# One query matmul per tile, one bank for the first half of K, three halvings of the second half, result matmuls at the head of the next value loop

## Chip, cores, metric

One core of one Trainium2 chip. The metric is the device time of one execution in microseconds (us), the median of several runs on the same chip.

## The reference

```python
B, H, Sq, Skv, Dh = 8, 32, 1, 4096, 128          # q, k, v in bf16
scale = q.shape[-1] ** -0.5
scores = jnp.einsum('bhqd,bhkd->bhqk', q, k) * scale
attn = softmax(scores, axis=-1)
return jnp.einsum('bhqk,bhkd->bhqd', attn, v)
```

Attention of a single query row for 256 heads: each head reads its own K and V (1 MB each) once and does little with them.

## The kernel before

32 tiles of 8 heads. In a tile a partition holds 256 of a head's rows (16 partitions per head), so K and V of a tile are 128 x 32768 bf16, 8.39 MB each. Three buffers of that size hold K and V in turn. VectorE multiplies K by the query in place and halves the rows by adding; TensorE sums what is left with an identity matrix into a PSUM bank of 512 columns, VectorE reduces the bank to scores. ScalarE makes the weights, and TensorE multiplies them with V in a loop that runs one tile later. The parts that the change touches:

```python
    def q_prep(t):
        x, p0 = divmod(t * G, P)                          # q_all: 128 partitions
        qh = ps_q.tile([G, D], F32, name="qh", tag="qp")
        nc.tensor.matmul(qh[:], lhsT=ident[:, p0 : p0 + G], rhs=q_all[:, x, :], ...)
        qg = q_pool.tile([G, D], BF16, name="qg", tag="qg")
        nc.scalar.activation(out=qg[:], in_=qh[:], func=ACT.Copy)
        qp = ps_q.tile([P, D], F32, name="qp", tag="qp")
        nc.tensor.matmul(qp[:], lhsT=heads[:]..., rhs=qg[:], start=True, stop=True)
        qb = q_pool.tile([P, 1, D], BF16, name="qb", tag="qb")
        nc.scalar.activation(out=qb[:, 0, :], in_=qp[:], func=ACT.Copy)
    ...
    def width_of(t, u):                                   # u: quarter of K
        return D // 4 if u >= NU // 2 and 0 < t < NT - 3 else D // 2
    def product(t, lo, hi):
        nc.vector.tensor_tensor(out=part, in0=part, in1=qb[:].to_broadcast(...), op=ALU.mult)
        nc.vector.tensor_tensor(... 0 : D // 2 ... + D // 2 : D ...)
        if width_of(t, lo // UC) < D // 2:
            nc.vector.tensor_tensor(... 0 : D // 4 ... + D // 4 : D // 2 ...)
    def sum_over_d(t, u):                                 # one bank per quarter of K
        ps = ps_s.tile([P, UC, DS], F32, name="ps", tag="ps")
        n = width_of(t, u) // DS
        for s in range(n):
            nc.tensor.matmul(ps[:], lhsT=ident[:], rhs=kt[:, u * UC : (u + 1) * UC, s * DS : (s + 1) * DS], ...)
    ...
        for t in range(NT):                               # cut: the steady tiles
            product(t, 0, 2 * Q)
            ...
            result_of(t - 2)
            q_prep(t + 2)
            sum_over_d(t, 0); sum_over_d(t, 1)
            product(t, 2 * Q, 3 * Q); sum_over_d(t, 2)
            scores_of(t, 0); scores_of(t, 1)
            product(t, 3 * Q, C); sum_over_d(t, 3)
            scores_of(t, 2)
            values_loop(t - 1)
            load("k", t + 1); load("v", t)
            scores_of(t, 3); weights_of(t); copy_of(t - 1)
```

## Time and profile before

| | before |
|---|---|
| time, median | 1251.86 us (1251.5 to 1251.9) |
| span of the profiled run | 1250.2 us |
| VectorE, TensorE, ScalarE busy | 82%, 63%, 13% |
| load queue busy | 99.5% of 16 DMA engines |
| one steady tile | 38.7 us |

The prediction shows the lines that carry this. Two more kinds matter for what follows, and the prediction passed over them. The first are small rows of the list of DMA queues (queue and kind: packets, MB, share of 16 engines' time): beside the loads (q1), the programs of the engines are fetched by DMA while they run. Kernel before:

```profile
q8 instruction: 15, 0.25, 0.1%
q14 instruction: 9, 0.07, 0.0%
```

0.1% of the time, 24 packets. The second is the end of the stream in windows of 1 us (columns: window, its length, busy time and instructions of each engine, TensorE clock, DMA share, GB/s). Kernel before:

```profile
1244.00:1245.00 1.00, 0.61 (x8) 0.21 (x8) 0.00 (x0) 0.00 (x0) 0.00 (x0) 1.00 0.50 183
1245.00:1246.00 1.00, 0.40 (x4) 0.10 (x4) 0.00 (x0) 0.12 (x1) 0.00 (x0) 1.00 0.16 56
1246.00:1247.00 1.00, 0.98 (x18) 0.98 (x18) 0.00 (x0) 0.48 (x1) 0.00 (x0) 1.00 0.01 4
```

The DMA share is a mean over 16 engines, so one engine at work is 0.06. The loads do not stop at once: the share falls over 3 us, and the last V rows land only when the last engine is done.

### The profile page before, as it was taken

The page shows a single profiled execution, that of the slowest core. Times are in us where ns is not written, and L with a number is a line of the kernel's source. Part 1 is how long each engine was busy: PE and PEld are TensorE (multiplying, and loading weights), DVE is VectorE, ACT ScalarE, POOL GpSimd, SP SyncE. Part 2 cuts the span into 40 slices and gives each one's busy share as a digit, 9 for nine tenths or more (in the row PEclk, how much of TensorE's full clock was granted, in tenths as well). Part 3 has the DMA queues.
Part 4 walks back from the last instruction along what each step waited for, and adds up shares of the span by engine and source line. Part 5 has one row for each costly group of instructions (what it writes and reads, how often), then busy time and mean ns, then how long its engine had stood idle before and what let it go on. Part 6 is the DMA issues. An engine that isn't in the chain of part 4 may idle for free. (4 is left out here: it accounts for less than half of the span.)

```text
span 1250.2 us, 10842 instructions
## 1 busy us (share of the span) xinstructions
PE 786.8 (63%) x3116; PEld 299.6 (24%) x3116; DVE 1021.9 (82%) x495; ACT 166.1 (13%) x433; POOL 4.5 (0%) x24
## 2 busy tenths in 40 slices
PE   3366567666576655766558665577655776556755
PEld 1122123222232222322223222222222222212222
DVE  7887987878977789777798777987779877798783
ACT  0111011111011110111101111011110111101111
POOL 1000000000000000000000000000000000000000
PEclk9987788777888778877788777887778878779867
DMA  9999999999999999999999999999999999999997
GB/s 405 436 436 435 434 436 432 436 430 428 426 437 436 429 435 434 434 435 436 436 434 432 424 437 437 432 430 428 436 437 434 430 433 434 430 435 421 427 446 329
DMA packets 11432, 537.33 MB, mean 430 GB/s; under 512 B 1808, under 2 KB 2064, under 8 KB 2320
## 3 DMA queue, kind: packets, MB, share of 16 engines
q1 hardware_dynamic: 11072, 536.94, 99.5%
q8 instruction: 15, 0.25, 0.1%
q10 hardware_dynamic: 336, 0.07, 0.0%
q14 instruction: 9, 0.07, 0.0%
HBM read 536.94 MB, written 0.07 MB: 430 GB/s over the span
## 5 line engine op out<-in xcount | busy, mean ns | idle before, releaser
L191 DVE TENSOR_TENSOR kt<-kt,qb 128x8192 bf16<-128x8192 bf16 (+1 forms) x99 | 560.9, 5665 | 146.6 <-DMA kt<-in_k_dram 139.9
L211 PE MATMUL ps<-kt,ident 128*128 128x512 bf16 x800 | 278.4, 511 | 389.9 <-DVE kt L199 299.7
L294 PE MATMUL av<-vt,w 128*32 x1740 | 425.5, 397 | 4.6
L194 DVE TENSOR_TENSOR kt<-kt 128x4096 bf16<-128x4096 bf16 (+1 forms) x99 | 288.8, 2917 | 3.4
L294 PEld LDWEIGHTS av<-vt,w 128*32 x1740 | 173.4, 100 | 262.4 <-issue 119.5
L211 PEld LDWEIGHTS <-ident 128*128 128x128 bf16 x800 | 95.7, 120 | 565.4 <-issue 527.9
L223 DVE TENSOR_REDUCE sc<-ps 128x64 f32<-128x512 f32 x128 | 85.3, 685 | 54.0 <-PE ps L211 54.0
L248 ACT ACTIVATE e<-sc,nmax 128x256 bf16<-128x256 f32 x32 | 16.3, 508 | 706.7 <-DVE nmax L242 706.7
L255 ACT ACTIVATE w<-e,mine 128x256 bf16<-128x256 bf16 x256 | 105.6, 495 | 1.1
L199 DVE TENSOR_TENSOR kt<-kt 128x2048 bf16<-128x2048 bf16 x56 | 68.6, 1225 | 1.9
L351 ACT ACTIVATE comb<-av 32x512 bf16<-32x512 f32 (+1 forms) x32 | 18.8, 586 | 329.0 <-PEq L284 321.4
L280 PE MATMUL av<-vt,w 128*32 128x512 bf16 x116 | 47.2, 499 | 14.6 <-issue 13.1
L371 PE MATMUL op<-comb,pick 32*16 32x128 bf16 (+1 forms) x128 | 12.1, 213 | 20.7 <-ACT comb L351 20.7
L280 PEld LDWEIGHTS av<-vt,w 128*32 128x32 bf16 x116 | 6.9, 100 | 55.2 <-issue 55.2
L177 PE MATMUL qp<-qg,heads 8*128 8x128 bf16 x32 | 7.0, 217 | 16.7 <-ACT qg L175 16.7
L371 PEld LDWEIGHTS <-pick 32*16 32x16 bf16 (+1 forms) x128 | 8.7, 83 | 27.7 <-issue 27.3
L322 PE MATMUL av<-vt,w 128*32 128x512 bf16 x188 | 13.7, 418 | 2.3 <-DMA vt<-in_v_dram 2.3
L235 DVE TENSOR_REDUCE pmax<-sc 128x1 f32<-128x256 f32 x32 | 13.4, 420 | 1.1
L175 ACT ACTIVATE qg<-qh 8x128 bf16<-8x128 f32 x32 | 8.5, 266 | 33.5 <-PE qh L171 33.5
L171 PE MATMUL qh<-q_all,ident 128*8 128x128 bf16 x32 | 7.2, 225 | 8.7 <-DMA q_all<-in_q_dram 8.3
L179 ACT ACTIVATE qb<-qp 128x128 bf16<-128x128 f32 x32 | 8.9, 278 | 9.7 <-PE qp L177 9.7
L237 DVE TENSOR_SCALAR spread<-same,pmax 128x32 f32<-128x32 f32 x32 | 7.7, 242 | 1.1
(31 smaller groups left out, 47.7 us busy)
## 6 DMA issues: line engine op xcount, KB each, us to landing
kt<-in_k_dram SPq DMA_DIRECT2D x4, 4096.0 KB, 24.3
kt<-in_k_dram SPq DMA_DIRECT2D x4, 2048.0 KB, 13.0
vt<-in_v_dram SPq DMA_DIRECT2D x1, 4096.0 KB, 33.9
vt<-in_v_dram SPq DMA_DIRECT2D x1, 2048.0 KB, 38.5
vt<-in_v_dram SPq DMA_DIRECT2D x1, 1024.0 KB, 40.5
vt<-in_v_dram SPq DMA_DIRECT2D x1, 512.0 KB, 41.3
vt<-in_v_dram SPq DMA_DIRECT2D x31, 25.8
kt<-in_k_dram SPq DMA_DIRECT2D x29, 28.3
```

Source lines behind the costliest of these rows:

```text
L191: nc.vector.tensor_tensor(out=part, in0=part, in1=qb[:].to_broadcast([P, hi - lo, D]), op=ALU.mult)
L194: nc.vector.tensor_tensor(out=part[:, :, 0 : D // 2], in0=part[:, :, 0 : D // 2], in1=part[:, :, D // 2 : D], op=ALU.add,)
L199: nc.vector.tensor_tensor(out=part[:, :, 0 : D // 4], in0=part[:, :, 0 : D // 4], in1=part[:, :, D // 4 : D // 2], op=ALU.add,)
L211: nc.tensor.matmul(ps[:], lhsT=ident[:], rhs=kt[:, u * UC : (u + 1) * UC, s * DS : (s + 1) * DS], start=(s == 0), stop=(s == n - 1),)
L223: made = nc.vector.tensor_reduce(out=scs[t][:, u * UC : (u + 1) * UC], in_=sums.pop((t, u))[:], axis=AX.X, op=ALU.add)
L248: nc.scalar.activation(out=e[:], in_=sc[:], func=ACT.Exp, bias=nmax[:, 0:1], scale=scale, accum_out=esums[t // R][:, t % R : t % R + 1],)
L255: nc.scalar.activation(out=w[:, :, g, :], in_=e_g, func=ACT.Copy, scale=mine[:, 0, g : g + 1])
L280: pe.matmul(av, lhsT=wf[:, i * nw : (i + 1) * nw], rhs=vf[:, i * nv : (i + 1) * nv], **how)
L294: pe.matmul(av, lhsT=wf[:, bass.ds(ow + i * nw, nw)], rhs=vf[:, bass.ds(ov + i * nv, nv)], start=False, stop=False,)
L322: nc.tensor.matmul(avs[t][j * AG : (j + 1) * AG, :], lhsT=w[:, i, :, :], rhs=vt[:, c0 : c0 + CB, :], start=(i < TG), stop=(j not in group[ ...
L351: nc.scalar.activation(out=comb[0:n, :, :], in_=av[0:n, :, :], func=ACT.Copy)
L371: nc.tensor.matmul(ops[n][:], lhsT=pick[0:e, m, r, :], rhs=comb[0:e, m, :], start=(r == 0 and m == 0), stop=(r == R - 1 and m == CB - 1 an ...
```

## The change

Its intent: fewer matmuls and copies (one query matmul instead of two, two sums per quarter of the second half of K instead of four, one PSUM bank and one reduction for the whole first half), in exchange for one more add per quarter, and a TensorE that starts the sums of the next tile without the result matmuls ahead of them. The query of a tile is also made one tile ahead instead of two. The diff, cut to its core:

```diff
-    q_n = q.rearrange("b h o d -> (b h o) d").rearrange("(x p) d -> p x d", p=P)
+    q_n = q.rearrange("b h o d -> (b h o) d").rearrange("(x p) d -> p x d", p=QP)      # QP = 32
-    heads = consts.tile([G, G, PH], BF16, name="heads")
+    heads = consts.tile([QP, QP, PH], BF16, name="heads")
     def q_prep(t):
-        ... matmul with ident, copy to qg, matmul with heads, copy to qb
+        x, h0 = divmod(t * G, QP)
+        qp = ps_q.tile([P, D], F32, name="qp", tag="qp")
+        nc.tensor.matmul(qp[:], lhsT=heads[:, h0 : h0 + G, :].rearrange("h g x -> h (g x)"), rhs=q_all[:, x, :], ...)
+        ... copy to qb
-        return D // 4 if u >= NU // 2 and 0 < t < NT - 3 else D // 2
+        return D // 8 if lo >= C // 2 and 0 < t < NT - 3 else D // 2
     def product(t, lo, hi):
+        n = D
+        while n > width_of(t, lo):
+            n //= 2
             nc.vector.tensor_tensor(
+                out=part[:, :, 0:n], in0=part[:, :, 0:n], in1=part[:, :, n : 2 * n], op=ALU.add
-    def sum_over_d(t, u):
+    def sum_over_d(t, lo, hi):
+        ds = BANK // (hi - lo)                             # 512 columns, whatever the rows
+        n = width_of(t, lo) // ds
-        e = o_pool.tile([P, C], BF16, name="e", tag="e")
+        e = o_pool.tile([P, C], BF16, name="e", tag="ec")
-        comb = o_pool.tile([P, CB, D], BF16, name="comb", tag="comb")
+        comb = o_pool.tile([P, CB, D], BF16, name="comb", tag="ec")
         with tc.tile_critical() as loop:
+            if t > 0:
+                result_of(t - 1)
...                                                        # w_last in the scores pool, the loop of tiles
```

More of the change, by code (lines that the diff above doesn't have):

```diff
@@ L43 @@
     scale = float(D) ** -0.5
-    UC = 64
-    DS = 512 // UC
-    NU = C // UC
+    BANK = 512
     CB = 4
@@ L49 @@
     NQ = NT // R
+    QP = 32
     TB = 32
@@ L53 @@
     assert (NV - 2 * EDGE) % LOOP == 0
-    assert LAST % CB == 0 and TG * AG == P and NH % P == 0 and P % G == 0 and TB % PH == 0 and C % CB == 0
-    q_n = q.rearrange("b h o d -> (b h o) d").rearrange("(x p) d -> p x d", p=P)
+    assert LAST % CB == 0 and TG * AG == P and NH % QP == 0 and QP % G == 0 and TB % PH == 0 and C % CB == 0
+    q_n = q.rearrange("b h o d -> (b h o) d").rearrange("(x p) d -> p x d", p=QP)
     o_n = out.rearrange("b h o d -> (b h o) d").rearrange("(n u x) d -> n x u d", u=OB, x=RG)
@@ L62 @@
     consts = ctx.enter_context(tc.tile_pool(name="consts", bufs=1))
-    q_pool = ctx.enter_context(tc.tile_pool(name="q_pool", bufs=3))
+    q_pool = ctx.enter_context(tc.tile_pool(name="q_pool", bufs=2))
     w_pool = ctx.enter_context(tc.tile_pool(name="w_pool", bufs=2))
@@ L72 @@
     ps_z = ctx.enter_context(tc.tile_pool(name="ps_z", bufs=1, space=bass.MemoryType.PSUM))
-    q_all = consts.tile([P, NH // P, D], BF16, name="q_all")
+    q_all = consts.tile([QP, NH // QP, D], BF16, name="q_all")
     ident = consts.tile([P, P], BF16, name="ident")
@@ L81 @@
     )
-    heads = consts.tile([G, G, PH], BF16, name="heads")
+    heads = consts.tile([QP, QP, PH], BF16, name="heads")
     nc.gpsimd.memset(heads[:], 0.0)
     nc.gpsimd.affine_select(
-        out=heads[:], in_=heads[:], pattern=[[-1, G], [0, PH]], compare_op=ALU.not_equal,
+        out=heads[:], in_=heads[:], pattern=[[-1, QP], [0, PH]], compare_op=ALU.not_equal,
         fill=1.0, base=0, channel_multiplier=1,
@@ L128 @@
     )
-    w_last = consts.tile([P, LAST, RG], BF16, name="w_last")
-    nc.gpsimd.memset(w_last[:], 0.0)
     loads = {}
@@ L168, in q_prep @@
     def q_prep(t):
-        x, p0 = divmod(t * G, P)
-        qh = ps_q.tile([G, D], F32, name="qh", tag="qp")
+        x, h0 = divmod(t * G, QP)
+        qp = ps_q.tile([P, D], F32, name="qp", tag="qp")
         nc.tensor.matmul(
-            qh[:], lhsT=ident[:, p0 : p0 + G], rhs=q_all[:, x, :], start=True, stop=True
-        )
-        qg = q_pool.tile([G, D], BF16, name="qg", tag="qg")
-        nc.scalar.activation(out=qg[:], in_=qh[:], func=ACT.Copy)
-        qp = ps_q.tile([P, D], F32, name="qp", tag="qp")
-        nc.tensor.matmul(qp[:], lhsT=heads[:].rearrange("g h x -> g (h x)"), rhs=qg[:], start=True, stop=True)
+            qp[:], lhsT=heads[:, h0 : h0 + G, :].rearrange("h g x -> h (g x)"), rhs=q_all[:, x, :],
+            start=True, stop=True,
+        )
         qb = q_pool.tile([P, 1, D], BF16, name="qb", tag="qb")
@@ L180, in q_prep, with width_of @@
         qbs[t] = qb
-    def width_of(t, u):
-        return D // 4 if u >= NU // 2 and 0 < t < NT - 3 else D // 2
+    def width_of(t, lo):
+        return D // 8 if lo >= C // 2 and 0 < t < NT - 3 else D // 2
     def product(t, lo, hi):
@@ L193, in product, with scores_of @@
         )
-        nc.vector.tensor_tensor(
-            out=part[:, :, 0 : D // 2], in0=part[:, :, 0 : D // 2],
-            in1=part[:, :, D // 2 : D], op=ALU.add,
-        )
-        if width_of(t, lo // UC) < D // 2:
+        n = D
+        while n > width_of(t, lo):
+            n //= 2
             nc.vector.tensor_tensor(
-                out=part[:, :, 0 : D // 4], in0=part[:, :, 0 : D // 4],
-                in1=part[:, :, D // 4 : D // 2], op=ALU.add,
+                out=part[:, :, 0:n], in0=part[:, :, 0:n], in1=part[:, :, n : 2 * n], op=ALU.add
             )
     sums = {}
-    def sum_over_d(t, u):
+    def sum_over_d(t, lo, hi):
         kt = loads["k", t]
-        ps = ps_s.tile([P, UC, DS], F32, name="ps", tag="ps")
-        n = width_of(t, u) // DS
+        ps = ps_s.tile([P, BANK], F32, name="ps", tag="ps")
+        ds = BANK // (hi - lo)
+        n = width_of(t, lo) // ds
         for s in range(n):
             nc.tensor.matmul(
-                ps[:], lhsT=ident[:],
-                rhs=kt[:, u * UC : (u + 1) * UC, s * DS : (s + 1) * DS],
+                ps[:], lhsT=ident[:], rhs=kt[:, lo:hi, s * ds : (s + 1) * ds],
                 start=(s == 0), stop=(s == n - 1),
             )
-        sums[t, u] = ps
+        sums[t, lo] = ps
     scs = {}
-    def scores_of(t, u):
-        if u == 0:
+    def scores_of(t, lo, hi):
+        if lo == 0:
             scs[t] = sc_pool.tile([P, C], F32, name="sc", tag="sc")
+        ps = sums.pop((t, lo))[:].rearrange("p (c s) -> p c s", c=hi - lo)
         made = nc.vector.tensor_reduce(
-            out=scs[t][:, u * UC : (u + 1) * UC], in_=sums.pop((t, u))[:], axis=AX.X, op=ALU.add
+            out=scs[t][:, lo:hi], in_=ps, axis=AX.X, op=ALU.add
         )
-        if u == NU - 1:
+        if hi == C:
             behind_loop(made)
@@ L259, in weights_of @@
         if t == NT - 1:
+            w_last = sc_pool.tile([P, LAST, RG], BF16, name="w_last", tag="sc")
+            nc.gpsimd.memset(w_last[:], 0.0)
+            ws["last"] = w_last
             for i in range(LAST // CB):
@@ L363, in last_rows @@
                 nc.tensor.matmul(
-                    ops[n][:], lhsT=w_last[:, i, :], rhs=loads["v", t][:, C - LAST + i, :],
+                    ops[n][:], lhsT=ws["last"][:, i, :], rhs=loads["v", t][:, C - LAST + i, :],
                     start=False, stop=(i == LAST - 1),
@@ L392, in store_of @@
             nc.scalar.dma_start(o_n[s, :, lo : u + 1, :], stages[s][:, lo : u + 1, :])
-    Q = C // 4
+    Q, HALF = C // 4, C // 2
     load("k", 0)
@@ L399 @@
         q_prep(0)
-        q_prep(1)
         for t in range(NT):
@@ L408 @@
                 load("v", t)
-            product(t, 0, 2 * Q if loop else Q)
-            if not loop:
-                sum_over_d(t, 0)
+            if loop:
+                product(t, 0, HALF)
+            else:
+                product(t, 0, Q)
+                sum_over_d(t, 0, Q)
             if 0 < t - 1 <= LT:
@@ L414 @@
                     norm_of(n)
-                if t > 1:
+                if t > LT:
                     result_of(t - 2)
-            if t + 2 < NT:
-                q_prep(t + 2)
+            if t + 1 < NT:
+                q_prep(t + 1)
             if loop:
-                sum_over_d(t, 0)
+                sum_over_d(t, 0, HALF)
             else:
-                product(t, Q, 2 * Q)
-            sum_over_d(t, 1)
-            if not loop:
-                scores_of(t, 0)
-            product(t, 2 * Q, 3 * Q)
-            sum_over_d(t, 2)
+                product(t, Q, HALF)
+                sum_over_d(t, Q, HALF)
+                scores_of(t, 0, Q)
+            product(t, HALF, HALF + Q)
+            sum_over_d(t, HALF, HALF + Q)
             if loop:
-                scores_of(t, 0)
-            scores_of(t, 1)
+                scores_of(t, 0, HALF)
+            else:
+                scores_of(t, Q, HALF)
             if t > 2 and t % R == 1:
                 recip_of(n)
-            product(t, 3 * Q, C)
-            sum_over_d(t, 3)
-            scores_of(t, 2)
+            product(t, HALF + Q, C)
+            sum_over_d(t, HALF + Q, C)
+            scores_of(t, HALF, HALF + Q)
             if loop:
@@ L441 @@
                 values_of(t - 1, 0, C)
-            scores_of(t, 3)
+            scores_of(t, HALF + Q, C)
             weights_of(t)
```

## The prediction

> **What bounds the kernel now.** I read the page first: busy shares, then the DMA rows and queues.
>
> ```profile
> span 1250.2 us, 10842 instructions
> ...
> PE 786.8 (63%) x3116; PEld 299.6 (24%) x3116; DVE 1021.9 (82%) x495; ACT 166.1 (13%) x433; POOL 4.5 (0%) x24
> ...
> DMA  9999999999999999999999999999999999999997
> ...
> q1 hardware_dynamic: 11072, 536.94, 99.5%
> ...
> HBM read 536.94 MB, written 0.07 MB: 430 GB/s over the span
> ```
>
> No compute engine is full: VectorE, the busiest, is idle 18% of the time. The queue that loads K and V is 99.5% busy, in every slice but the last. The bytes are fixed: K and V are each 8*32*4096*128*2 = 268.4 MB, 536.9 in all. So the transfers are the first suspect. A busy queue alone proves little, since a transfer can be issued late; so next the waits, and the timeline of one steady tile.
>
> ```profile
> DVE kt L191 <- DMA kt<-in_k_dram: 139.9, 28, 6.3
> ```
>
> VectorE waits for K data in 28 tiles, 139.9/28 = 5.0 us each time, and (a line further down that list) 54 us in all for TensorE. Per tile, from the timeline:
>
> ```profile
> 508.85 8.69 DVE L191 TENSOR_TENSOR kt<-kt,qb 128x16384 bf16<-128x16384 bf16 x1 [4.88 <-DMA kt<-in_k_dram]
> ...
> 519.14 0.33 SPq L158 DMA_DIRECT2D kt<-in_k_dram  x1
> ...
> 539.14 1.86 PE L211 MATMUL ps<-kt,ident 128*128 128x512 bf16 x4 [7.91 <-DVE kt L199]
> ...
> 541.04 0.33 SPq L158 DMA_DIRECT2D vt<-in_v_dram  x1
> ...
> 547.55 8.69 DVE L191 TENSOR_TENSOR kt<-kt,qb 128x16384 bf16<-128x16384 bf16 x1 [4.83 <-DMA kt<-in_k_dram]
> ```
>
> The reader is to see a clock: 547.55 - 508.85 = 38.70 us from one K landing to the next. In it one K tile and one V tile of 8.39 MB land: 16.78 MB / 38.70 us = 434 GB/s. The queue is never empty when a load is issued. V issued at 541.04 stands behind the K that lands at 547.55: margin 6.5 us. K issued at 519.14 stands behind the V issued at 502.29; section 6 of the page gives a median of 25.8 us from a V issue to its landing, so about 528.1: margin 9.0 us. These two margins, and VectorE's idle 4.8 us per tile, are what a change may eat before it shows. The chain that ended last says the same of the end:
>
> ```profile
> 1204.55 41.43 DMA vt<-in_v_dram
> ...
> 1246.02 0.83 PE op L363 x12
> 1246.85 0.22 PE op L371 x4
> 1247.08 0.24 PE op L363 x4
> ```
>
> The last V rows land at 1246; what follows is 4.2 us of matmuls, one scaling and the store. So time = start-up of some 2 us, a stream of 537 MB, and 4.2 us of tail.
>
> **What the Trainium skill says.** "DMA: Bandwidth & Descriptors", section "Where 436 GB/s comes from", puts the ceiling of the 16 SBUF ports at 435.2 GB/s and says elsewhere that HBM may bind at about 358. The trace agrees with the first (434 in the steady tile), not with the second. At 435.2 GB/s the bytes alone take 1233.8 us: only 16 us of the span can be saved while the bytes stay. "SBUF — State Buffer", section "SBUF: two separate sides", says that engines and DMA use disjoint ports, so less TensorE work shouldn't speed the stream; nothing in the trace before tests it. The same page (box under "Door 1: The DMA port swizzle") says that 16-byte lines are read at full rate with at least two hits per line. The old first-half matmuls read runs of 8 bf16 = 16 bytes and take 3.61/16 = 0.226 us at full clock; the new ones read runs of 4 = 8 bytes, four hits, so I expect no slowdown. "VectorE: DVE Perf Modes", section "The perf-mode tier table", has 1224 ns for a bf16 tensor_tensor of 2048; the trace has 1225.
>
> **The change part by part, for one of the 28 tiles 1 to 28 that use the narrow second half.**
>
> *Third halving.* Each quarter of the second half gets an add of 128x1024. The groups give 4412, 2292 and 1225 ns for 8192, 4096 and 2048 elements (the first a product, of the same rate); the steps are 2120 and 1067, so the next is about 534, and the new add about 0.69 us (estimate). Twice: +1.38 us VectorE, +38.7 us over 56.
>
> *One bank for the first half.* Sixteen matmuls stay sixteen: before 64/8 = 8 for each of two quarters, now 64/4 = 16 for the half. The two 512-element reductions become one: -0.685 us of VectorE, -19.2 over 28. VectorE net: +0.7 per tile, about 1041 us in all (83%).
>
> *Fewer sums.* A second-half quarter needs 16/8 = 2 matmuls instead of 4: -112 of 800. Four took 1.86 us at the end of the tile, so two take about 0.93.
>
> *Query.* One matmul and one copy instead of two of each: -32 matmuls (7 us of TensorE) and -32 copies of 0.266 us (8.5 us of ScalarE), none on the path that sets the end. In the head the first product may start some 0.6 us earlier (9.53 to about 8.9; -0.27 matmul, -0.27 copy, less one hand-over), but K of tile 2 was issued at 41.12 with K0, K1 and V0 (25.2 MB, 58 us at 434 GB/s, from about 2) still landing until about 60. The q load keeps its 64 KB and its place.
>
> *Result matmuls into the head of the next value loop.* Four matmuls, 0.38 us in the trace, leave the front of the next tile's sums and stand before the loop. Tiles stay equal; the loop ends 0.4 us later, and so the K issue.
>
> *Shared buffer of e and comb.* In the instruction order of the built kernel the exp of a tile now waits for PE's sequencer: comb is read inside the critical section of the loop, which is released at its end. So exp moves from 542.8 to about 557.8 + 0.4 in this tile, w is ready some 4 us later at about 562.2 (exp 0.5, accumulator 0.2, eight copies 3.3), and is needed by the next loop at 541.4 + 38.7 = 580.1. 18 us to spare. The scores buffer is written again by the first reduction of the next tile, near 568.5 + 0.7: 10 us after exp has read it.
>
> *Sum on the two issues.* From K landing to V issue: before 541.04 - 508.85 = 32.2 us. After: +1.38 - 0.64 (the pair of reductions took 1.28 together) - 0.93 = 32.0 us. The margin of 6.5 us stays. K issue: about 0.4 us later minus that 0.2, margin about 8.8 us. VectorE's wait for K falls from 4.9 to about 4.2 us. The stream never runs dry, so the steady tiles cost 38.7 us as before. The tail's instructions are the same; w_last is zeroed late (0.3 us on GpSimd, between the exp near 1234 and the copies at 1237.6). Effect on the end: 0.
>
> **Rivals.**
>
> *VectorE becomes the bound.* For: it is the only engine that gets more work. Against: it would need 4.8 us more per tile and gets 0.7. If the short adds cost double my estimate, it is 2.1: still hidden. Were it the bound by 1 us per tile, the time would be 1280.
>
> *The exp behind the loop stalls the next loop.* For: it is a new wait of about 15 us per tile, and ScalarE then has exp, w, comb and the query copy in one burst. Against: 18 us and 10 us of slack, worked out above. If the slack were wrong by the whole burst, about 4 us per tile on TensorE would first eat the 9 us of the K issue: still nothing. Only a loss above that shows.
>
> *Narrow 8-byte runs slow the first-half matmuls.* If they took twice the 5.3 us that sixteen took at the mixed clock, TensorE would be 2 us late for the third quarter's sums and on time for the fourth: nothing.
>
> *A gain.* Fewer matmuls and one hop less in the head would help if compute set the pace. Only the head and tail are open, and neither gets shorter: at best about 1 us, 1250.8.
>
> **Range and chances.** Predicted 1251.7 us against 1251.86: the same within the spread of three runs (0.4 us). The irregular part is the stream itself: some tiles take 39 to 40 us without a late issue (issues of V at 113.09 and 153.28 are 40.2 apart), by my sum some 4 us in all; another mix of them moves the end by 1 us or so. That gives 1250.3 to 1253.2. Faster by 2% would need 1226.8, under the 1233.8 of the bytes alone: chance 0.01, for an error in my reading. Slower by 2% needs 25 us, 0.9 us in each of 28 tiles beyond all the slack: 0.01.
>
> **What would show it.** Right: the queue busy 99% or more; 38.7 us between K landings; VectorE near 1041 us with waits for K of about 4.2 us in most tiles; adds of 1024 at 0.69 us; 688 sums; exp released by PE's sequencer about 15 us later than before; same last rows of the chain. Wrong: a waiting VectorE whose releaser is ScalarE or TensorE instead of the K load, a landing-to-landing time over 39 us in most tiles, or K loads with under 19.4 us from issue to landing, which would mean a queue that had run dry.

## The result and the profile after

| | before | after |
|---|---|---|
| time, median of 6 | 1251.88 us (1251.49 to 1252.03) | 1253.34 us (1252.94 to 1253.48) |
| span of the profiled run | 1250.2 | 1251.2 |

The ratio is 1.0012, 95% interval 0.9999 to 1.0025. (A ratio is the mean time of one kernel's fast runs over that of the other's of the same rounds, so not quite the ratio of the medians.) By the 2% measure it is the same time. But the six runs of one and of the other do not overlap, and 1253.34 lies 0.14 us above the top of the range I had given. The forecast was -0.2 us; the result is +1.5. So there is a cost of about 1.5 us that I had not seen. The page of the changed kernel:

```profile
span 1251.2 us, 10619 instructions
...
PE 737.9 (59%) x2972; PEld 283.4 (23%) x2972; DVE 1043.5 (83%) x522; ACT 153.1 (12%) x401; POOL 5.3 (0%) x24
...
q1 hardware_dynamic: 11072, 536.94, 99.4%
q8 instruction: 14, 0.23, 0.1%
...
q14 instruction: 10, 0.08, 0.0%
```

VectorE has 1043.5 us of work (1041 were forecast), and q14 has ten packets instead of nine. The two new groups on VectorE (line, engine, operation, output and input, count; busy time, mean ns; idle time before), changed kernel:

```profile
L189 DVE TENSOR_TENSOR kt<-kt 128x1024 bf16<-128x1024 bf16 x56 | 38.7, 692 | 1.9
...
L213 DVE TENSOR_REDUCE sc<-ps 128x128 f32<-128x512 f32 x29 | 19.8, 683 | 0.0
```

The third add takes 692 ns (0.69 us were forecast), the wider reduction 683 ns, as the old one. The waits, changed kernel (who waited for whom: us in total, times, longest):

```profile
ACT e L238 <- PEq L279: 957.0, 28, 38.3
...
DVE kt L183 <- DMA kt<-in_k_dram: 139.6, 29, 6.3
```

The exp now waits for the end of the value loop, as foreseen, and VectorE still waits for K and for nothing else of size. The same steady tile as in the prediction, from the timeline of the changed kernel:

```profile
508.92 8.69 DVE L183 TENSOR_TENSOR kt<-kt,qb 128x16384 bf16<-128x16384 bf16 x1 [4.87 <-DMA kt<-in_k_dram]
...
519.65 0.33 SPq L153 DMA_DIRECT2D kt<-in_k_dram  x1
519.74 0.51 ACT L238 ACTIVATE e<-sc,nmax 128x256 bf16<-128x256 f32 x1 [33.22 <-PEq L279]
...
541.14 0.33 SPq L153 DMA_DIRECT2D vt<-in_v_dram  x1
...
547.62 8.69 DVE L183 TENSOR_TENSOR kt<-kt,qb 128x16384 bf16<-128x16384 bf16 x1 [4.80 <-DMA kt<-in_k_dram]
```

From K landing to K landing 38.70 us, from K landing to V issue 32.22 us (32.2 before, 32.0 forecast), margin 6.5 us. Nothing in the tile has changed that could cost. The end, from the chain that ended last of the changed kernel:

```profile
1205.14 41.83 DMA vt<-in_v_dram
1246.97 0.04 issue
1247.01 0.83 PE op L360 x12
```

The last V rows land 1.0 us later than before (1247.0 against 1246.0); the tail behind them is the same. So the time was lost in the stream, in tiles that look alike. The windows at the end of the changed kernel show by whom:

```profile
1245.00:1246.00 1.00, 0.62 (x8) 0.21 (x8) 0.00 (x0) 0.00 (x0) 0.00 (x0) 1.00 0.18 67
1246.00:1247.00 1.00, 0.40 (x4) 0.10 (x4) 0.00 (x0) 0.13 (x1) 0.00 (x0) 1.00 0.07 25
```

A DMA share of 0.07 for a whole microsecond: one engine of sixteen is still loading while fifteen are done. The kernel before had 0.16 and then 0.01 in these two windows.

**The engines one by one.** The views show no single DMA engine, so what follows is read from the packet records of the trace themselves. Each load ends on each of its 16 engines with a packet of 4 bytes. Sorting these packets of the trace by time, sixteen belong to each load, and the first and last of them say how far the engines are apart. When which load has landed on its fastest and slowest engine (us):

```
                     second K tile    V of tile 1     first half of the last V    last V rows
before   fast/slow   41.45 / 41.76    99.51 / 101.20     1232.60 / 1236.21         1246.20
after    fast/slow   41.72 / 42.12    99.77 / 101.08     1232.94 / 1237.21         1247.20
```

The engines start together (0.3 us apart) and drift apart by 3.6 us before and 4.3 us after. Up to some 1000 us the drift comes in jumps of one engine at a time, right behind packets of q8 or q14. In the kernel before the slowest engine's distance goes 2.26 to 3.24 us behind the q14 packet at 706.6 and 3.24 to 4.22 behind that at 997.9: 0.98 us each. The packets show where it goes: the fetch at 706.6 takes 0.32 us, and the load packet of 64 KB that follows it on the same engine takes 3.08 us, where its neighbours take 2.42. That is 0.98 us together. Why the second packet is slow is not shown. The q14 packets of 8 KB at 146, 418, 707 and 998 us of the kernel before are 272 to 291 us apart, 7.0 to 7.5 tiles; the Trainium skill ("Runtime: NRT & Kernel Launch", section "Instruction fetch mechanics") puts 256 instructions into 16 KB, so 8 KB are by estimate 128, or 17 to 18 per tile, which is VectorE's number (15 to 16 operations and a branch or a semaphore). The runs below agree: 128, 256 and 512 instructions more bring one, two and four packets more. In the changed kernel such a series stands at 127, 379, 651, 901 and 1153 us: five instead of four. It is one and the same engine there: behind these five packets one engine's distance from the fastest goes from 0.2 to 1.2, from 1.2 to 2.2, from 2.2 to 3.2, from 3.1 to 4.1 and from 3.3 to 4.3 us, and each jump starts at about the distance at which the one before ended (between the last two the fastest lost ground, see dve_512_more). VectorE's built program has grown from 594 to 651 instructions, from 4.6 to 5.1 blocks of 128.

The Trainium skill, "Perfetto Trace Analysis", section "What 'DMA-bound' means", lists specific DMA engines as the first of the things that a DMA-bound kernel can be bound on. That is the case here, and a mean share of 99% hides it.

**Theory L.** A fetch of VectorE's instructions holds up the one DMA engine that carries it by about 1 us; all such fetches of VectorE fall on the same engine; as the queue is never empty, the lag is never made up, and the end waits for that engine. The third add makes a fifth fetch. **Rivals.** Q: the q load over 32 partitions is the loss (0.34 us of it, the mean over the sixteen engines, can be seen in the head, at the second K tile). E: the exp behind the loop, or the results in its head. W: the work of VectorE, not the length of its program.

### The profile page after: what moved, and what is told of

Read it like the earlier page. It is cut to its first block, busy times and chain, and to the rows that moved or that the text cites. A ratio compares the mean times of both kernels' runs of the same rounds, so it can differ in the third digit from the quotient of the medians.

```text
span 1251.2 us, 10619 instructions
## 1 busy us (share of the span) xinstructions
PE 737.9 (59%) x2972; PEld 283.4 (23%) x2972; DVE 1043.5 (83%) x522; ACT 153.1 (12%) x401; POOL 5.3 (0%) x24
## 5 line engine op out<-in xcount | busy, mean ns | idle before, releaser
L201 PE MATMUL ps<-kt,ident 128*128 128x512 bf16 x688 | 227.7, 484 | 472.9 <-DVE kt L189 472.5
L189 DVE TENSOR_TENSOR kt<-kt 128x4096 bf16<-128x4096 bf16 (+3 forms) x211 | 396.1, 1877 | 7.2
L291 PEld LDWEIGHTS av<-vt,w 128*32 x1740 | 183.2, 105 | 254.4 <-issue 87.3
L201 PEld LDWEIGHTS <-ident 128*128 128x128 bf16 x688 | 69.0, 112 | 613.1 <-DVE kt L189 503.8
L213 DVE TENSOR_REDUCE sc<-ps 128x64 f32<-128x512 f32 (+1 forms) x99 | 67.9, 686 | 31.1 <-PE ps L201 31.1
L368 PE MATMUL op<-comb,pick 32*16 32x128 bf16 (+1 forms) x128 | 18.3, 291 | 20.4 <-PE ps L201 12.4
L368 PEld LDWEIGHTS op<-comb,pick 32*16 32x16 bf16 x112 | 8.7, 109 | 38.2 <-issue 38.2
L166 PE MATMUL qp<-q_all,heads 32*128 32x128 bf16 x32 | 7.0, 220 | 11.4 <-DMA q_all<-in_q_dram 8.7
L319 PEld LDWEIGHTS <-w 128*32 128x32 bf16 x188 | 6.5, 109 | 9.6 <-issue 6.2
L232 DVE TRANSPOSE_TENSOR_REDUCE nmax<-spread 128x1 f32<-128x32 f32 x32 | 6.8, 212 | 1.1
```

Source lines behind the costliest of these rows:

```text
L189: nc.vector.tensor_tensor(out=part[:, :, 0:n], in0=part[:, :, 0:n], in1=part[:, :, n : 2 * n], op=ALU.add)
L201: nc.tensor.matmul(ps[:], lhsT=ident[:], rhs=kt[:, lo:hi, s * ds : (s + 1) * ds], start=(s == 0), stop=(s == n - 1),)
L213: made = nc.vector.tensor_reduce(out=scs[t][:, lo:hi], in_=ps, axis=AX.X, op=ALU.add)
L291: pe.matmul(av, lhsT=wf[:, bass.ds(ow + i * nw, nw)], rhs=vf[:, bass.ds(ov + i * nv, nv)], start=False, stop=False,)
L319: nc.tensor.matmul(avs[t][j * AG : (j + 1) * AG, :], lhsT=w[:, i, :, :], rhs=vt[:, c0 : c0 + CB, :], start=(i < TG), stop=(j not in group[ ...
L368: nc.tensor.matmul(ops[n][:], lhsT=pick[0:e, m, r, :], rhs=comb[0:e, m, :], start=(r == 0 and m == 0), stop=(r == R - 1 and m == CB - 1 an ...
```

## The experiments

Each kernel was timed five times (halves_whole_again six) beside the kernel before on the same chip; quoted is the median and its distance from the median of before in the same rounds. Every result agreed with the reference. Distances under 0.3 us are not read. The 95% intervals of the ratios are about 0.13% wide on each side, so of the single steps only those of 2 us and more exclude 1; what is rested on is ranges of runs that do not overlap, and the landing times in the traces.

### Parts of the change

**after_q_old**: the changed kernel with the old query path.

```diff
-    q_all = consts.tile([QP, NH // QP, D], ...)          # 32 partitions, one matmul, one copy
+    q_all = consts.tile([P, NH // P, D], ...)            # 128 partitions, two matmuls, two copies
```

> The changed kernel with the old query path (q loaded over 128 partitions, two small matmuls per tile). In the changed kernel's trace every DMA engine is 0.34 us later than before from the first K tile on, right behind the q load; the lag of the slowest engine against the fastest before the last V chunks is 4.27 us instead of 3.61. Theory L (an instruction fetch holds up the one DMA engine that carries it by about 1 us, VectorE's 8 KB fetches all fall on one engine, and VectorE's longer program needs five of them instead of four): the 0.34 us comes back, the fifth fetch stays: 1252.9 to 1253.1, lag still 4.1 to 4.4, five VectorE fetches. Rival Q (the q load is the whole loss): 1251.9. Rival E (the exp behind the loop, or the results in its head): 1253.3, nothing comes back.

Measured: 1252.50 us (1252.46 to 1252.69), +0.73. The second K tile lands at 41.39 / 41.74, as before. Five VectorE fetches; slowest engine 4.07 us behind; last V rows at 1246.99. More came back than the 0.34 us, so it lies below the 1252.9 to 1253.1 of L as well, but half the loss stayed: Q isn't the whole.

**after_two_halvings**: the changed kernel, narrowed twice instead of three times.

```diff
-        return D // 8 if lo >= C // 2 and 0 < t < NT - 3 else D // 2
+        return D // 4 if lo >= C // 2 and 0 < t < NT - 3 else D // 2
```

> The changed kernel with two halvings instead of three: VectorE's program falls from 651 to 595 instructions, as long as before. Theory L: four VectorE fetches of 8 KB, slowest engine about 1 us less behind, but the q load's 0.34 us stays: 1252.2 to 1252.4. Rival Q or E: 1253.3.

Measured: 1251.91 us (1251.72 to 1252.00), +0.14. Four VectorE fetches, last V rows at 1246.30. It keeps the exp behind the loop and the new q load, and loses nothing that can be read: E is out. It is below the 1252.2 to 1252.4 that L expected, as the q load's 0.4 us, visible in the head again (41.76 / 42.20), did not reach the end.

**halving_alone**: the kernel before with the third add.

```diff
-        return D // 4 if u >= NU // 2 and 0 < t < NT - 3 else D // 2
+        return D // 8 if u >= NU // 2 and 0 < t < NT - 3 else D // 2
     def product(t, lo, hi): ...
+            nc.vector.tensor_tensor(... 0 : D // 8 ... + D // 8 : D // 4 ...)
```

> The kernel before with the third halving alone (650 VectorE instructions): Theory L: a fifth VectorE fetch and nothing else: 1252.6 to 1252.9, the K and V stream as early as before in the head, lag of the slowest engine about 4.3. Rivals Q and E: 1251.9.

Measured: 1252.35 us (1252.27 to 1252.76), +0.58. Five VectorE fetches, last V rows at 1247.25 in the profiled run, which was the slowest of the five (1252.76). Less than the 0.7 to 1.0 expected, but clear of the kernel before except for one of its nine runs (1252.32).

**results_alone**: the kernel before with the result matmuls at the head of the next loop and the buffer of e and comb shared.

```diff
         with tc.tile_critical() as loop:
+            if t > 0:
+                result_of(t - 1)
```

> The kernel before with the result matmuls in the head of the next loop and the shared buffer of e and comb alone (594 VectorE instructions as before): Theory L and Rival Q: 1251.9 within 0.3, though the exp waits for the loop's end in all steady tiles. Rival E: 1252.5 to 1253.3.

Measured: 1251.90 us (1251.47 to 1252.12), +0.13: nothing. Last V rows at 1245.93.

**bank_alone**: the kernel before with one bank for the first half (and the query made one tile ahead, as in the changed kernel).

```diff
+                sum_over_d(t, 0, HALF)
-                sum_over_d(t, 0); sum_over_d(t, 1)
```

> The kernel before with the one bank for the first half alone (and w_last in the scores pool); VectorE has 28 reductions fewer but more semaphore instructions, 595 in all. Theory L: four VectorE fetches, 1251.6 to 1252.1. If narrower reads of K by TensorE or the wider reduction cost anything at the end, more.

Measured: 1251.47 us (1251.36 to 1251.63), -0.08: nothing. Four fetches, last V rows at 1246.00. It lies just under the expected 1251.6 to 1252.1, as the kernel before did in these rounds (1251.55). Reads of K in runs of 8 bytes cost nothing at the end.

### The suspected cost by itself

**dve_128_more, dve_256_more, dve_512_more**: the kernel before with 4, 8 or 16 memsets of one column per tile, in the time in which VectorE waits for K.

```diff
             weights_of(t)
+            for _ in range(4):                           # 8, 16
+                nc.vector.memset(idle[:], 0.0)           # 128 x 1
```

> The kernel before with four memsets of 128x1 on VectorE behind each tile's weights, in its idle time: 128 instructions more (722), that is one block of 8 KB at 64 bytes each. Theory L: one more VectorE fetch (five), the slowest DMA engine 1 us later: 1252.7 to 1253.0. Rival W (what costs is VectorE's work, not the length of its program): the memsets are some 10 us of work in all, inside 4.8 us of idle time per tile: 1251.9.

Measured: 1252.78 us (1252.40 to 1252.95), +1.03.

> Eight such memsets per tile: 256 instructions more (850). Theory L: six VectorE fetches, 1253.6 to 1254.0, lag of the slowest engine about 5.5. Rival W: 1251.9.

Measured: 1253.82 us (1253.60 to 1253.86), +2.07, ratio 1.0016 (1.0003 to 1.0030).

> The kernel before with sixteen memsets of 128x1 on VectorE per tile: 512 instructions more (1106, 8.6 blocks of 128). Theory L: eight VectorE fetches instead of four, the slowest DMA engine four times 0.98 us later: 1255.2 to 1256.0. Rival W: 1251.9, for the memsets take about 1 us of the 4.8 us in which VectorE waits for K.

Measured: 1255.95 us (1255.68 to 1256.48), +4.40, ratio 1.0037 (1.0024 to 1.0051). VectorE's fetches are 5, 6 and 8 in these traces; in the last they stand at 78, 224, 380, 533, 669, 820, 969 and 1120 us. From the page of dve_512_more:

```profile
span 1253.9 us, 11354 instructions
...
PE 788.4 (63%) x3116; PEld 298.9 (24%) x3116; DVE 1050.8 (84%) x1007; ACT 166.0 (13%) x433; POOL 4.4 (0%) x24
...
q14 instruction: 13, 0.11, 0.0%
```

29 us more work on VectorE, 1 us per tile where it waited for 4.8, 0.04 MB more on q14, and 4.4 us more time. The memsets of a tile and the wait behind them, from the timeline of dve_512_more:

```profile
504.50 1.95 DVE L446 MEMSET idle<- 128x1 f32 x16
509.45 8.69 DVE L192 TENSOR_TENSOR kt<-kt,qb 128x16384 bf16<-128x16384 bf16 x1 [3.00 <-DMA kt<-in_k_dram]
```

W is out: this work lay in idle time, of which 3.00 us were left, and the third add, with 38.7 us of work, cost less. The end of the stream of dve_512_more, in windows:

```profile
1247.00:1248.00 1.00, 0.79 (x11) 0.27 (x9) 0.00 (x0) 0.00 (x0) 0.00 (x0) 1.00 0.15 55
1248.00:1249.00 1.00, 0.59 (x8) 0.19 (x8) 0.00 (x0) 0.00 (x0) 0.00 (x0) 1.00 0.06 25
1249.00:1250.00 1.00, 0.54 (x7) 0.23 (x7) 0.00 (x0) 0.28 (x1) 0.00 (x0) 1.00 0.07 25
```

One engine alone for 2 us. By 0.98 us per fetch it would be about 4 (an estimate) if the others had kept their pace. They did not. The next V load waits for the last sums of a K tile (541.00 in the tile shown, the issue at 541.04), and that tile has to land on all sixteen engines first, so the issue comes ever closer to the moment at which the fastest engine is free for it. In the kernel before the V issue at 541.04 is 3.7 us ahead of that moment (544.70), with the slowest engine 2.3 us behind; the one at 1084.85 is 1.7 us ahead (1086.57), with the slowest 4.2 behind. There the first load packet on the fastest engine takes 2.99 us instead of 2.42, and its next landing comes after 19.83 us instead of 19.35: it has begun to wait. In dve_512_more the steps of the fastest engine behind a V issue are 19.38 to 19.95 us from 620 us on. The load that has landed on the fastest engine at 931.75 us in the kernel before lands there at 933.77 in this one, and on the slowest 4.0 us later. So the whole stream then goes at the pace of the slowest.

**act_256_more**: 256 instructions more on ScalarE instead.

```diff
             weights_of(t)
+            for _ in range(8):
+                nc.scalar.activation(out=idle[:], in_=same[:, 0:1], func=ACT.Copy)   # 128 x 1
```

> The kernel before with eight copies of 128x1 on ScalarE behind each tile's weights: 256 instructions more on ScalarE (707), VectorE as before. Theory L: two more 8 KB fetches fall on another DMA engine than VectorE's, one that is behind it by 1 us or more, so the end moves by 0 to 0.8 us: 1251.9 to 1252.7. If any longer program cost 1 us per block, 1253.9.

Measured: 1252.88 us, but from 1252.05 to 1253.49, the widest of all; +1.13, a miss of the expected 0 to 0.8. The stream behaved as expected: two more q14 packets, last V rows at 1246.05 as before. What was lost came after it: the sixth packet of ScalarE's series runs from 1248.19 to 1248.74, in the tail, and one of the sixteen packets of the final store starts at 1248.73, 0.2 us behind the others. So here the fetch met the store. In the profiled run (1252.38 us, +0.63) all of the loss lies there: from the last V rows to the end of the span it has 4.52 us, the kernel before 3.95. For the slower four runs, and for the store as its cause, that is not shown.

### The query path again

**after_again** and **after_q_old_again**: the changed kernel and after_q_old, in the same rounds.

> The changed kernel once more, so that it is timed on the same chip and in the same rounds as the next two. Theory L: 1253.1 to 1253.5, five VectorE fetches. If the 1253.34 was a matter of that chip, it falls to 1252.6 or less.

Measured: 1253.09 us (1252.65 to 1253.51), +1.54, five VectorE fetches: the loss is not a matter of the chip.

> The changed kernel with the old query path once more, beside it: so far it was 0.7 us above the kernel before, and the changed kernel 1.46 above. If the query path costs only the 0.34 us that the head shows, the difference between these two runs is 0.2 to 0.5 us; if the 0.84 us holds in the same rounds, 0.7 to 1.0.

Measured: 1252.43 us (1252.28 to 1252.59), +0.88. The difference of 0.66 us (0.73 the first time, as the difference of the distances from before) holds, between the two expected ranges: the query path costs about 0.7 us here, more than its 0.34 in the head.

**after_third** and **after_q_padded**: the changed kernel, and the same with a second small matmul and copy per query, so that TensorE and ScalarE have their old number of instructions, and the new q load.

```diff
     def q_prep(t):
+        qh = ps_q.tile([G, D], F32, name="qh", tag="qp")
+        nc.tensor.matmul(qh[:], lhsT=ident[0:QP, h0 : h0 + G], rhs=q_all[:, x, :], ...)
+        nc.scalar.activation(out=qb[0:G, 0, :], in_=qh[:], func=ACT.Copy)     # overwritten below
```

> The changed kernel, as partner in the same rounds: 1253.0 to 1253.4.

Measured: 1253.03 us (1252.90 to 1253.16), +1.48.

> The changed kernel with a second small matmul and a second small copy per query again (3172 and 483 instructions on TensorE and ScalarE, as with the old query path; 651 on VectorE), but q still loaded over 32 partitions. If the rest of the query path's cost is the place of other fetches (the changed kernel has one of 8 KB and one of 16 KB after the last V row), 1252.7 to 1252.9. If the load over 32 partitions is all of it, as the changed kernel: 1253.0 to 1253.4.

Measured: 1252.61 us (1252.48 to 1252.78), +1.06. Work was added to the changed kernel and it became 0.42 us faster, its runs all below those of after_third. So of the query path's 0.7 us some 0.4 go with the matmul and copy left out, not with the load.

The traces show where in time the 0.7 us lie. Not in the head: at the load that lands at 197 us the mean of the sixteen engines is 196.88 in the changed kernel and 196.84 in the kernel before, and the kernels with the old query path are scattered from 196.65 to 197.12. The last V rows land some 0.2 us later with the new path (1247.17 to 1247.27, against 1246.99 and 1247.03 in after_q_old), which may be scatter: halving_alone, with the old path, has 1247.25. The rest comes behind them. From the last V rows to the end of the span there are 4.03, 4.36 and 3.84 us in the three traces of the changed kernel, 3.83 in both of after_q_old and 3.84 in after_q_padded. (The profiled runs of after_again and after_q_old_again are 0.66 us apart: 0.14 in the landing, 0.53 behind it.) In the changed kernel one fetch of 8 KB and one of 16 KB fall behind the last V rows (at 1247.9 and 1248.2 in the first trace), in the other two kernels none does. But the third trace of the changed kernel has both fetches too, and its tail is as short as theirs. So that these fetches are the cause is not shown.

### A version with a shorter program

**halves_whole**: the changed kernel with the old query path and two halvings, and the second half of K in one piece like the first: VectorE's program has 480 instructions.

```diff
-            product(t, HALF, HALF + Q); sum_over_d(t, HALF, HALF + Q)
-            product(t, HALF + Q, C); sum_over_d(t, HALF + Q, C)
+            product(t, HALF, C); sum_over_d(t, HALF, C)
```

> The changed kernel with the old query path and two halvings, and the second half of K in one piece as the first: 480 VectorE instructions instead of 594. Theory L: three VectorE fetches instead of four, and the slowest engine 1 us earlier than in the kernel before, unless another engine then is the last: 1250.9 to 1251.4. Rivals Q, E, W: 1251.9.

Measured: 1251.16 us (1251.13 to 1251.42), -0.59.

> The kernel with three VectorE fetches once more: 0.4 to 0.8 us under the kernel before, as the first time (0.59).

Measured: 1251.09 us (1250.95 to 1251.24), -0.46; no run of it is above the fastest of before (1251.34) in these rounds. From the page of halves_whole:

```profile
span 1249.7 us, 10768 instructions
...
q14 instruction: 8, 0.07, 0.0%
```

Three VectorE fetches, at 165, 539 and 903 us; last V rows at 1245.67 and 1245.22. It beats both kernels, by 0.04% and 0.15%. (It differs from the kernel before in more than the length of its program, so by itself it is no proof of theory L; it is a forecast of L that came true.)

### All together

```
                    VectorE   VectorE   slowest engine,         last V    time minus
                    instr.    fetches   half of the last V      rows      before
halves_whole(,again)  480        3      1235.67, 1235.22        1245.67, 1245.22      -0.59, -0.46
before                594        4      1236.21                 1246.20                0
bank_alone            595        4      1236.00                 1246.00               -0.08
results_alone         594        4      1235.93                 1245.93               +0.13
after_two_halvings    595        4      1236.32                 1246.30               +0.14
act_256_more          594        4      1236.06                 1246.05               +1.13
halving_alone         650        5      1237.26                 1247.25               +0.58
after_q_old(,again)   651        5      1236.99, 1237.02        1246.99, 1247.03      +0.73, +0.88
dve_128_more          722        5      1236.86                 1246.86               +1.03
after_q_padded        651        5      1237.22                 1247.21               +1.06
after (3 times)       651        5      1237.21, 1237.18, .29   1247.20, 1247.17, .27 +1.46, +1.54, +1.48
dve_256_more          850        6      1238.13                 1248.12               +2.07
dve_512_more         1106        8      1240.05                 1250.05               +4.40
```

The last landing falls into groups by the number of VectorE fetches alone, whatever else the kernel does: 1245.2 to 1245.7, 1245.9 to 1246.3, 1246.9 to 1247.3, 1248.1, 1250.05. From four to eight it is 3.85 us, 0.96 per fetch. The medians follow less closely, as they also hold what comes after the last V rows: to the end of the span there are 3.8 us in most traces, but 4.0 to 4.5 in some (4.36 in after_again, 4.52 in act_256_more). And each landing is that of one profiled run, not of the median.

## Why the prediction was wrong

Right were the bound, the clock of the tile and most costs on the compute engines: the third add (692 ns), VectorE's total (1043.5 against 1041), 688 sums, the exp behind the loop with no effect (results_alone), the narrow reads without penalty (sixteen first-half matmuls take 3.63 us, before 3.61), the V issue 32.2 us behind K, the tail's instructions. VectorE's wait for K stayed at 4.8 us in the tile shown, where 4.2 were forecast, because VectorE's wait for the last sums fell from 1.35 to 0.53 us, which I had counted in the V issue and not here. Smaller misses: the four result matmuls take 0.59 us in their new place (0.38 forecast), two sums 1.04 (0.93), and the first product starts at 9.29 (8.9). None of them matters here. The prediction's 1233.8 us for the bytes alone is an estimate from the figure that it cites, not a measurement. The rivals that I had named did not happen.

The step that failed is the last of the sum: "The stream never runs dry, so the steady tiles cost 38.7 us as before. [...] Effect on the end: 0." It has two faults.

- The term that was mis-sized is the third halving. It was priced as 38.7 us of VectorE time, hidden, at 0. By its length in instructions (594 to 651, past five blocks of 128) it adds one fetch, about 1 us on the DMA engine that ends last: the last V rows land at 1247.25 instead of 1246.20 with the third halving alone (+0.58 in the median), and at 1246.99 and 1247.03 in the changed kernel without its query path (+0.73 and +0.88).
- "The q load keeps its 64 KB and its place" and "none on the path that sets the end" left out a second cost. With three halvings the new query path costs about 0.7 us; with two it costs nothing that can be read (after_two_halvings, +0.14). About 0.2 us of it are in the landing of the last V rows; the rest, where a trace shows it, comes behind them, in a tail of which I had said that its instructions are the same. They are, but it took up to 4.36 us instead of 3.95. What makes it longer stays open.

Behind both lies one reading: I took 16 DMA engines for one queue, because the share was 99.5%. The margin of 6.5 us has the same fault: it was measured to the start of VectorE, which waits for the slowest engine. To the fastest engine it was 3.7 us in that tile and 1.7 us for the issue at 1084.85; it shrinks as the lag grows. And the range's explanation, "The irregular part is the stream itself [...] another mix of them moves the end by 1 us or so", named the place without looking at it. The tile of 40.2 us that I quoted for it is no accident of the stream: behind a 16 KB fetch at 97.2 us one engine lands V of tile 1 at 101.20, the other fifteen by 99.84; K of tile 3, next in the queue, lands on it at 120.55, on the others by 119.32, and VectorE starts that tile with the sixteenth. That irregularity is made by the program, so it was to be counted, not to be put into the width of a range.

## What to carry to other kernels

In this kernel, whose loads are issued so far ahead that the queue never drains, a DMA engine does not make up what it loses, and the stream ends with the slowest of the sixteen: look at when a load lands on its first and last engine, not at the mean share. In that state the length of a program in instructions can be a cost even on an engine with idle time (here 1 us per 128 instructions of VectorE, measured over a range from 480 to 1106), so few large instructions are better than many small ones. The price goes by whole blocks: 650 and 722 instructions both have five fetches, and the last V rows land at 1247.25 and 1246.86 (the medians, +0.58 and +1.03, differ more). It holds for the program whose fetches fall on the last engine: 256 instructions more on ScalarE brought two fetches more and left the last V rows at 1246.05. Effects of this size (0.1%) need runs in the same rounds; a dose that is doubled twice settled in three runs what single undo experiments left within their noise.

## What the Trainium skill lacked or had wrong

- "Runtime: NRT & Kernel Launch", section "Instruction fetch mechanics", gives the refill as blocks of 16 KiB and calls the cost of crossing one "mostly hidden". The q8 packets are 16 KB in every trace here (TensorE's by all appearance: they stay at 15 when VectorE or ScalarE alone gets more instructions, and are 14 in the changed kernel with its 2972 matmuls instead of 3116), but those of q14 behind the start, VectorE's among them, are 8 KB, one per 128 instructions. And with a full load queue the cost is not hidden: 0.98 us on the DMA engine that carries one (0.32 for the packet, 0.66 more for the load packet behind it), and 0.96 us per fetch at the end from four to eight fetches.
- The same section doesn't say on which DMA engine a fetch falls. In these runs VectorE's all added to the lag of one engine (its distance grew 2.26, 3.24, 4.22 us in the kernel before).
- No page says how the distance between the engines adds up over an unbroken stream, which was decisive here: from 0.3 us in the second K tile to 3.6 us before the end, and at about 4 us the fast ones wait for the slow.
- No page gives the price of an 8 KB fetch near a 16-packet store at the end; one run had a store packet 0.2 us late behind such a fetch, with times that varied by 1.4 us.
